# One group of resident blocks instead of two, and an earlier, smaller first table of units

## The chip, the cores and the metric

The kernel runs on one core of a Trainium2 chip. Its time is the device time of one execution in microseconds (us); of several runs the median is given. Engines are named as in the profile: PE is the tensor engine's matmul (PEld its weight load), ACT the scalar engine, DVE the vector engine, POOL the GpSimd engine, and SP the engine that issues most of the transfers.

## The reference

A gated linear recurrence over four sequences of 3648 tokens with 256 channels, and a two-level mixture of experts on its output (4 groups of 4 experts, one expert for each token):

```python
# B, S, D = 4, 3648, 256
a_base = 1.0 / (1.0 + np.exp(-a_param))
log_a = 8.0 * sigmoid(r_gate) * np.log(np.clip(a_base, 1e-06, 1.0 - 1e-06))
a_t = np.exp(log_a)
x_gated = np.sqrt(np.maximum(1.0 - a_t * a_t, 1e-06)) * sigmoid(i_gate) * x
for t in range(S):
    h = a_t[:, t] * h + x_gated[:, t]
    y[:, t] = h
# x = y.reshape(14592, 256)
g_idx = argmax(x @ w_group);  g_w = softmax weight of g_idx
for each group g, for its tokens xg:
    e_idx = argmax(xg @ w_expert[g]);  e_w = softmax weight of e_idx
    for each expert e of the group, for its tokens:      # w1: 256x1024, w2: 1024x256
        out[tokens] = (g_w * e_w) * (relu(x @ w1[g, e]) @ w2[g, e])
```

## The kernel before

The tokens come in 16 chunks of up to 1024 (`SIZES`: 4, then 13 times 8, then 4 and 2 tiles of 128 tokens); chunks are counted from 0 in the code and by words (first, second) in the text. A chunk is loaded with channels on the partitions in two halves. ACT computes tanh (`tanh_r`), exp (`decay`), square, square root (`norm`) and the input gate (`gate_i`) for each half; DVE multiplies (`gated`, `scale_s`) and runs the recurrence (`scan`). Square root and exp need different tables on ACT, so each change of function costs a table load.

*Rows.* PE turns the scanned chunk to rows of tokens and computes the routing logits in the same products (`rows1`, two tiles of 128 tokens to a call: eight products on PE's timeline, 128x148 each). They land in PSUM, and ACT copies them to SBUF (`rows2`). The PSUM has eight banks: `q_r` has two buffers of one bank, `q_h` two of one bank, `q_y` and `q_o` one buffer of two banks each; the rows take `q_y` and `q_o` in turn.

*Routing.* DVE finds each token's expert and its place in the expert's list (`route1`, `route3`, `weigh`, `route4`; ACT's `route2` is an exponential over d_; PE's `rank` counts over tiles with tri and ones; pi holds the places). POOL then writes the rows to the lists in DRAM (`scatter`, tensor y_s), one indirect transfer for each tile.

*Blocks and units.* Work on experts starts before all tokens are routed. (1) Four experts (0, 4, 8, 12, `RES`) have their weights resident. After the chunks in `RSTAGES` a block of up to 128 tokens of each is computed in plain fp32 (`add_blocks`: `rows_block` is the gather that SP issues, `turn_block`, `copy_block`, `mm1_block`, `relu_block`, `mm2_block`, `finish_block`, `give_block`). (2) After the chunks in `STAGES` a table is made on DVE of so many units, a unit being 256 tokens of one expert (`early`, `table`, then three small products on PE, `in_row1`, and `in_row2` on DVE). Its entries are registers for SP: which weights to load, which rows to gather. The first 12 units (`add_native`) split w1 into two parts in fp32r (`split_halves`: ACT makes w1h, DVE w1l) and take w2 in plain fp32; later ones (`add_unit`) split both. A unit's rows are gathered by SP (`gather`, g<-y_s), turned by PE (`turn_native`), copied by ACT (xh) and DVE (xl, `rest_halves`). (3) After the last chunk a table of pairs follows (`tP`, the number of its units is fixed at `NPS`), and (4) a tail for each of the 16 experts, of two blocks of 128 tokens or three, by the count that is left. The buffers of the resident weights become those of the units' weights.

*Order.* Each engine's order is fixed when the program is built: `Plan.run` places every operation by a model with a cost for each operation, a hop between engines (`HOP`, `hop`), a rate and delays for transfers, buffers that come free (`Ring`), and a due time (SOON is at once). Operations of one engine, and the transfers issued by SP and POOL, run in the order in which the plan placed them. `order=` adds an order without data.

In the profile all matmuls but the transposes have the line of the helper `matmul`: L249.

Of the kernel before, what the change touches and what calls it, by code (L numbers as in the profile page):

```python
# [45 lines left out]
class Plan:  # L46


    HOP = 0.14
    RATE, LAG, FAR = 400e3, 2.0, 4.0  # L50
    COOL, WARM = 2.7, 3.4
    TABLE, TURN = 1.28, 2.0
    SLACK, RUSH = 0.02, 0.3
# [24 lines left out]
        return o  # L78

    def hop(self, a, b):  # L80
        return self.HOP if a.dma or a.engine != b.engine else 0.0 if a.engine == "PE" else 0.1

    def ready(self, ring):
        if len(ring.given) < ring.n:
# [19 lines left out]
    def place(self, o, t):  # L104
        e, us = o.engine, o.cost
        if e == "ACT" and o.table and o.table != self.table:
            us, self.table = us + self.TABLE, o.table
        if e == "PE":
            if t - self.clock[e] > self.COOL:
                self.cold = self.WARM  # L110
            us += min(us, self.cold / 2)
            self.cold = max(0.0, self.cold - us)
        end = self.clock[e] = t + us
        if o.dma:
            self.wire = max(self.wire, end) + o.dma / self.RATE
            end = self.wire + self.LAG if e == "SP" else end + self.FAR
        for b in o.new:
            b.ring.given.append(b)
        for b in o.new + o.use:
            b.left -= 1  # L120
            b.free = max(b.free, end + self.HOP)
        for n in o.next:
            n.wait -= 1
        for n in o.then:
            n.wait -= 1
            n.at = max(n.at, end + self.hop(o, n))
# [31 lines left out]
def rglru_moe_kernel(ctx: ExitStack, tc: tile.TileContext, x, r_gate, i_gate, a_param,  # L158
# [20 lines left out]
    SIZES = [4] + [8] * 13 + [4, 2]   # L179
    CH = 8  # L180

    RES, RSTAGES = (0, 4, 8, 12), (1, 2)
    STAGES = [(4, 8), (7, 9), (10, 9)]
    NATIVE = 12
    HALVES = range(0, NATIVE)

# [17 lines left out]
    STEP2, STEPB, STEPN = 10.5, 7.2, 13.4  # L204
    FIRST = range(1, 5)
    URGENT = (0, 1, 2, 3, 4, 7)
    ORES = 60
    HASTE, SPLIT, PREP, WAHEAD = 8, 8, 12, 25
    IF = 0.3

# [17 lines left out]
    def buf(n):  # L228
        return Buf(rings[n])
# [18 lines left out]
    def matmul(*a, **k):  # L248
        last[0] = T.matmul(*a, **k).ins.name  # L249
# [139 lines left out]


    def rows1(ck, i):
        q = ck.t["qy", i] = pools[ck.qy(i)].tile([P, 2, 512], F32, name=ck.qy(i))
        for k in range(2):
            for h in range(2):
                matmul(q[:, k, h * P:h * P + YW], lhsT=ck.t["a", h][:, (2 * i + k) * P:(2 * i + k + 1) * P],
                         rhs=yw[:, h, :], start=h == 0, stop=h == 1, skip_group_check=True)

    def rows2(ck, i):
        if i % 2 == 0:
            ck.t["yo", i // 2] = pools["wf"].tile([P, 4 * DW], F32, name="wf").rearrange("p (k c) -> p k c", c=DW)  # L400
        S.copy(ck.t["yo", i // 2][:, i % 2 * 2:i % 2 * 2 + 2, :], ck.t["qy", i][:, :, 0:DW])  # L401
# [143 lines left out]
    def act(n):  # L545
        return 0.16 + n / 1180
# [4 lines left out]
    def add_chunk(ck, before):  # L551
        K, W, due, b = ck.K, ck.W, ck.due, ck.b
        ld = {}
        for what in "asx":
            for h in range(2):
                if ck.c:
                    at = due + LOADS[what] + 3 * h
                    ld[what, h] = op("SP", 0.06, lambda what=what, h=h: load(ck, what, h), at,
                                     new=[b[what, h]], dma=W * P * 4, soon=at - AHEAD)
                else:  # L560
                    ld[what, h] = None
                    b[what, h].ring.given.append(b[what, h])
        sq = {}
        for h in range(2):
            th = op("ACT", act(W), lambda h=h: tanh_r(ck, h), due + h * OTURN, [ld["a", h]], use=[b["a", h]], table="exp")
            de = op("ACT", act(W) + 0.18, lambda h=h: decay(ck, h), due + h * OTURN, [th], use=[b["a", h]], table="exp")
            sq[h] = op("ACT", act(W), lambda h=h: square(ck, h), due + h * OTURN, [de], [b["v", h]], [b["a", h]])
            if ck.c < 2:
                plan.either(sq[h], "DVE", dve(W), lambda h=h: square(ck, h, True))
        n2 = op("ACT", 2 * act(W), lambda: norm(ck), due + ONORM, [sq[0], sq[1]], use=[b["v", 0], b["v", 1]], table="sqrt")  # L570
        ga = []
        for h in range(2):
            gi = op("ACT", act(W), lambda h=h: gate_i(ck, h), due + OGATE, [ld["s", h]], use=[b["s", h]], table="exp")
            ga.append(op("DVE", dve(W), lambda h=h: gated(ck, h), due + OGATED, [gi, ld["x", h]], use=[b["s", h], b["x", h]]))
        ck.sc = []
        for h in range(2):
            ms = op("DVE", dve(W), lambda h=h: scale_s(ck, h), due + OSCAN + OH * h, [ga[h], n2], use=[b["s", h], b["v", h]])
            sc = op("DVE", 0.1 + W / 455, lambda h=h: scan(ck, h, before), due + OSCAN + 1 + OH * h,
                    [ms] + ([before.sc[h]] if before else []), use=[b["a", h], b["v", h]] + ([before.b["a", h]] if before else []))
            ck.sc.append(sc)  # L580

        urgent = SOON if ck.c in URGENT else 0.0
        rdue = due + OROWS + (SOON if ck.c in FIRST else 0.0) + (ck.c == 0) * STEP1
        ck.qy = lambda i: "q_o" if ck.c < 6 and i % 2 else "q_y"
        ck.y, yos, r1s = [], [], []
        r0 = []
        u = K / CH
        early = ck.c <= STAGES[-1][0]

        def at(o):  # L590
            return due + (ROUTE if early else o) + urgent
        for i in range(K // 2):
            q = buf(ck.qy(i))
            r1 = op("PE", 1.1, lambda i=i: rows1(ck, i), rdue + 2 * i, ck.sc, [q], [b["a", 0], b["a", 1]])
            if i % 2 == 0:
                yos.append(buf("wf"))
            yo = yos[-1]
            r2 = op("ACT", 0.62, lambda i=i: rows2(ck, i), rdue + 2 * i, [r1], [yo] if i % 2 == 0 else [], [q] + ([yo] if i % 2 else []),
                    order=ACTWF[-1:])
            ACTWF.append(r2)  # L600
            ck.y.append(r2)
            if i % 2 == 1 or i == K // 2 - 1:
                r1s.append(chain(route1(ck, i // 2), [0.23, 0.23], at(OROUTE[0]), ck.y[i // 2 * 2:] + r1s[:1],
                                 [b["d"]] if i < 2 else [], [yo] + ([b["d"]] if i >= 2 else []))[1])
                ck.routed = plan.ops[-2]
                r0.append(op("POOL", 0.25, lambda i=i // 2: rows3(ck, i), at(OROUTE[0]), r1s[-1:], use=[yo]))
        r3a, r3 = chain(route3(ck), [0.32, 0.31, 0.32, 0.38, 0.42, 0.17], at(OROUTE[2]), r1s, [b["oe"]], [b["d"]])
        r2 = op("ACT", 0.34, lambda: route2(ck), at(OROUTE[1]), [r3a], (), [b["d"]], table="exp")
        _, rw = chain(weigh(ck), [0.31, 0.18, 0.18, 0.17, 0.15, 0.3], at(OROUTE[2]) + OW, [r2, r3], use=[b["d"]] + yos)
        q = buf("q_y")  # L610
        rk = op("PE", 0.15, lambda: rank(ck), at(ORANK), [r3, before and before.acc], [q], [b["oe"]], order=[before and before.hold])
# [85 lines left out]
    def in_row2(tb, n):  # L697
        q = tb.q
        er = small([1, n])
        tb.act = small([1, n], I32)  # L700
        V.tensor_scalar(er, q[0:1, :n], float(NE - 1), None, op0=ALU.min)
        yield
        V.tensor_scalar(tb.act, q[0:1, :n], float(NE) - 0.5, None, op0=ALU.is_lt)
        yield
        tb.ei = small([1, n], I32)
        V.tensor_copy(tb.ei, er)
        yield
        tb.chg = small([1, n], I32)
        V.tensor_tensor(tb.chg[:, 2:], er[:, 2:], er[:, :n - 2], op=ALU.not_equal)
# [758 lines left out]
```

## Time and profile before

| | us |
|---|---|
| median of 3 runs | 899.62 (898.64 to 902.72) |
| profiled execution, its own time | 901.76 |
| its span, first to last instruction | 900.0 |
| busy: PE, DVE, ACT, POOL | 833.2, 656.4, 606.8, 307.0 |
| first product of unit 0 on PE | 149.13 |
| first results of units 0, 11, 36 on ACT | 168.63, 348.72, 648.18 |
| first result of the last tail | 888.36 |

Busy PE time is modelled, since products are pipelined: the step from the start of one row to the start of the next says what a product costs. A row of the timeline gives start, duration, engine, line, operation, out<-in, shape, the count that was merged, and in brackets the idle time of the engine ahead of it with what ended it. Positions in time are microseconds from the first instruction.

### The profile page before, as it was taken

The page shows a single profiled execution, that of the slowest core. Times are in us where ns is not written, and L with a number is a line of the kernel's source. Part 1 is how long each engine was busy: PE and PEld are TensorE (multiplying, and loading weights), DVE is VectorE, ACT ScalarE, POOL GpSimd, SP SyncE. Part 2 cuts the span into 40 slices and gives each one's busy share as a digit, 9 for nine tenths or more (in the row PEclk, how much of TensorE's full clock was granted, in tenths as well). Part 3 has the DMA queues.
Part 4 walks back from the last instruction along what each step waited for, and adds up shares of the span by engine and source line. Part 5 has one row for each costly group of instructions (what it writes and reads, how often), then busy time and mean ns, then how long its engine had stood idle before and what let it go on. Part 6 is the DMA issues. An engine that isn't in the chain of part 4 may idle for free.

```text
span 900.0 us, 18908 instructions
## 1 busy us (share of the span) xinstructions
PE 833.2 (93%) x6274; PEld 809.9 (90%) x6274; DVE 656.4 (73%) x1345; ACT 606.8 (67%) x901; POOL 307.0 (34%) x290
## 2 busy tenths in 40 slices
PE   2348999999999999999999999999999999999994
PEld 1238998999999899999999999999999999999994
DVE  5796888888889766887777777767766667666681
ACT  8996999999999736556565555556554555555561
POOL 2255753672863467321111111111211213122132
PEclk9968999999999999999999999999999999999997
DMA  9979968988977468857677677688665556555420
GB/s 301 419 286 395 343 224 304 414 302 325 401 264 275 159 240 275 261 180 251 218 232 228 221 232 230 221 273 268 196 190 173 178 183 209 153 178 180 136 72 23
DMA packets 74462, 216.28 MB, mean 240 GB/s; under 512 B 10709, under 2 KB 28895, under 8 KB 71776
## 3 DMA queue, kind: packets, MB, share of 16 engines
q1 hardware_dynamic: 62464, 183.61, 61.4%
q0 software_dynamic: 11872, 31.10, 9.0%
q8 instruction: 66, 1.08, 0.5%
q14 instruction: 60, 0.49, 0.2%
HBM read 182.76 MB, written 34.00 MB: 241 GB/s over the span
## 4 chain that ended last, share of the span: by engine, by line
PE 79%; DMA 6%; ACT 6%; issue 6%; DVE 2%; POOL 1%; SPq 0%; POOLq 0%; DVEq 0%; ACTq 0%
PE q_o L249 37%; PE q_h L249 29%; PE q_y L249 9%; PE q_r L889 2%; DMA a<-in_r_gate_dram 1%; POOL out_dram L1011 1%; DMA i<-in_i_gate_dram 1%; DMA x<-in_moe_w_dram 1%; ACT v L367 1%; ACT wf L401 1%; DMA x<-in_x_dram 1%; DMA y_s<-wf,pi 1%; DMA out_dram<-o,cl 1%; ACT L367 1%; ACT a L348 1%
## 5 line engine op out<-in xcount | busy, mean ns | idle before, releaser
L1011 POOL DMA_INDIRECT out_dram<-o,cl x122 | 138.1, 1132 | 439.0 <-ACT o L1003 240.7
L249 PE MATMUL q_h<-xh,w1h 128*128 128x256 f32 (+1 forms) x720 | 191.2, 294 | 1.5 <-ACT xh L1131 1.5
L502 POOL DMA_INDIRECT y_s<-wf,pi x114 | 145.8, 1279 | 84.0 <-issue 37.9
L249 PE MATMUL q_h<-xl,w1h 128*128 128x256 f32 x592 | 166.8, 282 | 0.0
L249 PE MATMUL q_h<-xh,w1l 128*128 128x256 f32 x592 | 166.8, 282 | 0.0
L249 PE MATMUL q_o<-w2h,hh 128*128 128x256 f32 x784 | 158.2, 334 | 1.2 <-DVE o L1005 0.8
L249 PEld LDWEIGHTS q_o<-w2h,hh 128*128 128x128 f32 x784 | 124.7, 190 | 9.3 <-DVE o L1005 1.0
L249 PEld LDWEIGHTS q_h<-xh,w1h 128*128 128x128 f32 x720 | 128.6, 193 | 2.5 <-ACT xh L1131 1.7
L917 ACT ACTIVATE hh<-q_h 128x512 fp32r<-128x512 f32 x100 | 60.1, 602 | 92.7 <-PE q_h L249 82.7
L249 PEld LDWEIGHTS q_h<-xl,w1h 128*128 128x128 f32 x592 | 111.7, 189 | 0.6
L249 PEld LDWEIGHTS q_h<-xh,w1l 128*128 128x128 f32 x592 | 111.7, 189 | 0.0
L920 DVE SCALAR_TENSOR_TENSOR hl<-q_h,hh 128x512 fp32r<-128x512 f32 x100 | 68.8, 688 | 48.3 <-ACT hh L917 48.1
L249 PE MATMUL q_y<-yw,a 128*128 128x148 f32 x368 | 59.3, 305 | 33.4 <-DVE a L388 25.4
L249 PEld LDWEIGHTS q_y<-yw,a 128*128 128x128 f32 x368 | 53.7, 201 | 36.9 <-issue 19.8
L249 PE MATMUL q_o<-w2l,hh 128*128 128x256 f32 x464 | 78.7, 295 | 0.0
L249 PEld LDWEIGHTS q_o<-w2l,hh 128*128 128x128 f32 x464 | 66.4, 188 | 1.4
L388 DVE TENSOR_TENSOR_SCAN a<-a,v 128x1024 f32<-128x1024 f32 (+8 forms) x38 | 67.4, 1791 | 0.0
L868 DVE TENSOR_TENSOR w1l<-x,w1h 128x1024 fp32r<-128x1024 f32 x50 | 61.0, 1220 | 6.7 <-ACT w1h L866 4.8
L249 PE MATMUL q_o<-w2h,hl 128*128 128x256 f32 x400 | 64.4, 283 | 0.0
L917 ACT ACTIVATE a<-q_y 128x384 fp32r<-128x384 f32 (+1 forms) x64 | 24.9, 442 | 57.3 <-issue 29.5
L1005 DVE TENSOR_SCALAR o<-q_o,cl 128x256 f32<-128x256 f32 x53 | 25.6, 483 | 51.6 <-ACT o L1003 33.4
L868 DVE TENSOR_TENSOR w2l<-x,w2h 128x1024 fp32r<-128x1024 f32 x50 | 60.5, 1216 | 2.8 <-ACT w2h L866 2.8
(336 smaller groups left out, 1861.7 us busy)
## 6 DMA issues: line engine op xcount, KB each, us to landing
x<-in_moe_w_dram SPq DMA_DIRECT2D x100, 512.0 KB, 4.6
wf<-in_moe_w_dram SPq DMA_DIRECT2D x64, 512.0 KB, 4.0
w2h<-in_moe_w_dram SPq DMA_DIRECT2D x14, 1024.0 KB, 8.0
a<-in_r_gate_dram SPq DMA_DIRECT2D x26, 512.0 KB, 9.6
i<-in_i_gate_dram SPq DMA_DIRECT2D x26, 512.0 KB, 9.1
x<-in_x_dram SPq DMA_DIRECT2D x26, 512.0 KB, 8.9
w2l<-in_moe_w_dram SPq DMA_DIRECT2D x24, 512.0 KB, 7.9
g<-y_s SPq DMA_DIRECT2D x37, 276.0 KB, 4.5
```

Of the source, the lines that this page charges most:

```text
L249: last[0] = T.matmul(*a, **k).ins.name
L348: S.activation(a, a, AF.Tanh, scale=0.5)
L367: S.activation(v, v, AF.Sqrt, scale=-0.25, bias=quarter)
L388: V.tensor_tensor_scan(a[:, sl], a[:, sl], v[:, sl], init, ALU.mult, ALU.add)
L401: S.copy(ck.t["yo", i // 2][:, i % 2 * 2:i % 2 * 2 + 2, :], ck.t["qy", i][:, :, 0:DW])
L502: ins = G.indirect_dma_start(out=y_s, out_offset=bass.IndirectOffsetOnAxis(ap=ck.pi[:, k:k + 1], axis=0), in_=ck.t["yo", k // 4][:, k % 4, ...
L868: V.tensor_tensor(lo[m.b][:, sl], src, hi[m.b][:, sl].bitcast(F32), op=ALU.subtract)
L889: T.transpose(m.qx[:, h * P:(h + 1) * P], m.g[:, h, c * X1:c * X1 + P], ident)
L917: S.activation(hh, q, AF.Relu)
L920: V.scalar_tensor_tensor(hl, q, 0.0, hh.bitcast(F32), op0=ALU.max, op1=ALU.subtract)
L1005: V.tensor_scalar(o, m.qo[h], m.col("cw", h), None, op0=ALU.mult)
L1011: ins = G.indirect_dma_start(out=out, out_offset=bass.IndirectOffsetOnAxis(ap=m.col("idx", h), axis=0), in_=m.o[h], in_offset=None, bounds ...
```

## The change

`RSTAGES` loses the second group of four blocks (after the third chunk). `STAGES` puts a table of two units after the fourth chunk and one of six after the fifth, in place of eight after the fifth; the later tables of nine stay. `NPS` grows by two, which keeps the number of token places: four blocks fewer, two units more. The second chunk's rows (`SPREAD`) use `q_y` and `q_o` for the first four tiles and two single banks each of `q_h` and `q_r` for the last four, so ACT copies those in four pieces. Ahead of them PE gets four products of 296 columns whose result is not used (`warm`), due once the scale of the second half is done. The third chunk's square root on ACT is ordered behind the second chunk's routing exponential. A few figures of the planner's model differ: the hop on one engine, when a POOL transfer has landed, the cost of a scatter of the first four chunks, the due time of the blocks.

```diff
-    RATE, LAG, FAR = 400e3, 2.0, 4.0
+    RATE, LAG, NEAR, FAR = 400e3, 2.0, 2.4, 4.0
...
-        return self.HOP if a.dma or a.engine != b.engine else 0.0 if a.engine == "PE" else 0.1
+        return self.HOP if a.dma or a.engine != b.engine else 0.0 if a.engine == "PE" else 0.04
...
         if o.dma:
+            far = end + self.NEAR + min(self.FAR, max(0.0, self.wire - end))
             self.wire = max(self.wire, end) + o.dma / self.RATE
-            end = self.wire + self.LAG if e == "SP" else end + self.FAR
+            end = self.wire + self.LAG if e == "SP" else far
...
-    RES, RSTAGES = (0, 4, 8, 12), (1, 2)
-    STAGES = [(4, 8), (7, 9), (10, 9)]
+    RES, RSTAGES = (0, 4, 8, 12), (1,)
+    STAGES = [(3, 2), (4, 6), (7, 9), (10, 9)]
...
-    NPS = 37 - NA
+    NPS = 39 - NA
...
-    ORES = 60
+    ORES = 55
+    HEAT = 4
+    SPREAD = (1,)
...
     def rows1(ck, i):
-        q = ck.t["qy", i] = pools[ck.qy(i)].tile([P, 2, 512], F32, name=ck.qy(i))
+        n = ck.qy(i)
+        q = ck.t["qy", i] = ([pools[n].tile([P, 512], F32, name=n) for _ in range(2)] if n in ("q_h", "q_r") else
+                             pools[n].tile([P, 2, 512], F32, name=n))
...
+    def warm(n):
+        q = pools["q_r"].tile([P, 512], F32, name="q_r")
+        for _ in range(n):
+            matmul(q[:, 0:2 * YW], lhsT=ident, rhs=yw.rearrange("p h w -> p (h w)"), start=True, stop=True)
...
-        S.copy(ck.t["yo", i // 2][:, i % 2 * 2:i % 2 * 2 + 2, :], ck.t["qy", i][:, :, 0:DW])
+        q, k = ck.t["qy", i], i % 2 * 2
+        if type(q) is list:
+            for n in range(2):
+                S.copy(ck.t["yo", i // 2][:, k + n, :], q[n][:, 0:DW])
+        else:
+            S.copy(ck.t["yo", i // 2][:, k:k + 2, :], q[:, :, 0:DW])
...
-        n2 = op("ACT", 2 * act(W), lambda: norm(ck), due + ONORM, [sq[0], sq[1]], use=[b["v", 0], b["v", 1]], table="sqrt")
+        n2 = op("ACT", 2 * act(W), lambda: norm(ck), due + ONORM, [sq[0], sq[1]], use=[b["v", 0], b["v", 1]], table="sqrt",
+                order=[before.exps] if ck.c == 2 else ())
...
+        if ck.c == 1:
+            plan.op("PE", 0.5 * HEAT, lambda: warm(HEAT), due + OSCAN + SOON, [ms], [buf("q_r")])
...
-        ck.qy = lambda i: "q_o" if ck.c < 6 and i % 2 else "q_y"
+        ck.qy = lambda i: ("q_h", "q_r")[i % 2] if ck.c in SPREAD and i > 1 else "q_o" if ck.c < 6 and i % 2 else "q_y"
...
-            ck.sca.append(op("POOL", 1.3 * n, ...
+            ck.sca.append(op("POOL", (1.65 if ck.c < 4 else 1.3) * n, ...
```

What this does to the order shows in three places. In each name the last number tells buffers apart; w1h_175 to w2l_182 are the resident weights of the four experts, w1 and w2 of each.

First, PE from the third chunk's rows to the first product of block 0 (rows are products of yw and a; tri and ones are the rank; hl is a block's gathered rows). Before:

```order
L249 MATMUL q_y<-yw,a 128x148 x4
L249 MATMUL q_o<-yw,a 128x148 x4
L249 MATMUL q_y<-yw,a 128x148 x4
L249 MATMUL q_o<-yw,a 128x148 x4
L249 LDWEIGHTS tri
L249 MATMUL q_y<-cn,tri 128x16
L249 LDWEIGHTS ones
L249 MATMUL q_y<-cacc,ones 128x16
L1127 MATMUL q_r<-yw,hl 128x128 x4
L249 LDWEIGHTS ones
L249 MATMUL q_y<-cacc,ones 128x16
L249 MATMUL q_h<-xh,w1h_175 128x128 x8
```

After:

```order
L252 MATMUL q_o<-yw,a 128x148 x4
L252 MATMUL q_y<-yw,a 128x148 x4
L252 MATMUL q_o<-yw,a 128x148 x4
L252 MATMUL q_y<-yw,a 128x148 x4
L252 MATMUL q_o<-yw,a 128x148 x4
L252 LDWEIGHTS tri
L252 MATMUL q_y<-cn,tri 128x16
L252 LDWEIGHTS ones
L252 MATMUL q_y<-cacc,ones 128x16
L1146 MATMUL q_r<-yw,hl 128x128 x4
L252 MATMUL q_h<-xh,w1h_175 128x128 x16
```

The third chunk's rank and block 0 now stand behind the fourth chunk's four groups of rows as well, which came within block 0 before.

Second, PE ahead of unit 0 (its first product is the one with w1h_1408, now w1h_974; g is a unit's gathered rows, t are the table's columns). Before:

```order
L249 MATMUL q_h<-xh,w2h_181 128x128 x16
L249 MATMUL q_y<-yw,a 128x148 x4
L249 MATMUL q_o<-w2l_182,hh 128x256 x4
L249 LDWEIGHTS tri
L249 MATMUL q_y<-cn,tri 128x16
L249 LDWEIGHTS ones
L249 MATMUL q_y<-cacc,ones 128x16
L249 MATMUL q_o<-w2l_182,hh 128x256 x4
L249 MATMUL q_h<-xh,w1h_1408 128x256
```

After:

```order
L252 MATMUL q_o<-w2l_182,hh 128x256 x8
L252 LDWEIGHTS tri
L252 MATMUL q_y<-cn,tri 128x16
L252 LDWEIGHTS ones
L252 MATMUL q_y<-cacc,ones 128x16
L1102 MATMUL q_r<-yw,g 128x128 x8
L252 LDWEIGHTS ones
L252 MATMUL q_y<-cacc,ones 128x16
L252 MATMUL q_y<-yw,t_1192 1x128
L252 MATMUL q_y<-yw,t_1193 1x128
L252 MATMUL q_y<-yw,t_1213 128x128
L252 MATMUL q_h<-xh,w1h_974 128x256
```

Between block 3 and unit 0 there stand now the fifth chunk's rank, the turns of units 0 and 1, and the count and the row products of the fifth chunk's table.

Third, DVE ahead of unit 0's xl, the last operand of its first products. Before:

```order
L388 SCALAR_TENSOR_TENSOR a<-a,v 128x640
L388 SCALAR_TENSOR_TENSOR a<-a,v 128x384
L1057 TENSOR_TENSOR w1l_1436<-w2l_1379,w1h_1408 128x1024
L526 TENSOR_TENSOR cl<-g,mA_1249 128x4
L527 TENSOR_SCALAR cl<-cl 128x2
L1065 TENSOR_TENSOR xl<-q_r,xh 128x512
```

After:

```order
L702 SCALAR_TENSOR_TENSOR t_1193<-t_1192,t_1193 128x1
L703 TENSOR_SCALAR t_1193<-t_1193 128x1
L784 TENSOR_TENSOR t_1221<-t_1186,t_1190 128x16
L786 TENSOR_SCALAR t_1221<-t_1221 128x16
L788 TENSOR_TENSOR t_1221<-t_1221,t_1186 128x16
L790 SCALAR_TENSOR_TENSOR done<-t_1221,done 128x16
L1084 TENSOR_TENSOR xl<-q_r,xh 128x512
```

The table of the fifth chunk, 24 steps of which the last six are shown, now stands directly ahead of xl.

More of the change, by code (lines that the diff above doesn't have):

```diff
@@ L391, in rows1 @@
     def rows1(ck, i):
-        q = ck.t["qy", i] = pools[ck.qy(i)].tile([P, 2, 512], F32, name=ck.qy(i))
+        n = ck.qy(i)
+        q = ck.t["qy", i] = ([pools[n].tile([P, 512], F32, name=n) for _ in range(2)] if n in ("q_h", "q_r") else
+                             pools[n].tile([P, 2, 512], F32, name=n))
         for k in range(2):
             for h in range(2):
-                matmul(q[:, k, h * P:h * P + YW], lhsT=ck.t["a", h][:, (2 * i + k) * P:(2 * i + k + 1) * P],
+                matmul((q[k] if type(q) is list else q[:, k])[:, h * P:h * P + YW], lhsT=ck.t["a", h][:, (2 * i + k) * P:(2 * i + k + 1) * P],
                          rhs=yw[:, h, :], start=h == 0, stop=h == 1, skip_group_check=True)
+    def warm(n):
+        q = pools["q_r"].tile([P, 512], F32, name="q_r")
+        for _ in range(n):
+            matmul(q[:, 0:2 * YW], lhsT=ident, rhs=yw.rearrange("p h w -> p (h w)"), start=True, stop=True)
     def rows2(ck, i):
@@ L592, in add_chunk @@
         for i in range(K // 2):
-            q = buf(ck.qy(i))
-            r1 = op("PE", 1.1, lambda i=i: rows1(ck, i), rdue + 2 * i, ck.sc, [q], [b["a", 0], b["a", 1]])
+            q = [buf(ck.qy(i)) for _ in range(1 + (ck.qy(i) in ("q_h", "q_r")))]
+            r1 = op("PE", 1.1, lambda i=i: rows1(ck, i), rdue + 2 * i, ck.sc, q, [b["a", 0], b["a", 1]])
             if i % 2 == 0:
@@ L597, in add_chunk @@
             yo = yos[-1]
-            r2 = op("ACT", 0.62, lambda i=i: rows2(ck, i), rdue + 2 * i, [r1], [yo] if i % 2 == 0 else [], [q] + ([yo] if i % 2 else []),
+            r2 = op("ACT", 0.62 + 0.1 * (len(q) - 1), lambda i=i: rows2(ck, i), rdue + 2 * i, [r1], [yo] if i % 2 == 0 else [], q + ([yo] if i % 2 else []),
                     order=ACTWF[-1:])
@@ L607, in add_chunk @@
         r3a, r3 = chain(route3(ck), [0.32, 0.31, 0.32, 0.38, 0.42, 0.17], at(OROUTE[2]), r1s, [b["oe"]], [b["d"]])
-        r2 = op("ACT", 0.34, lambda: route2(ck), at(OROUTE[1]), [r3a], (), [b["d"]], table="exp")
+        ck.exps = r2 = op("ACT", 0.34, lambda: route2(ck), at(OROUTE[1]), [r3a], (), [b["d"]], table="exp")
         _, rw = chain(weigh(ck), [0.31, 0.18, 0.18, 0.17, 0.15, 0.3], at(OROUTE[2]) + OW, [r2, r3], use=[b["d"]] + yos)
@@ L617, in add_chunk @@
             step = [] if n == 1 else None
-            ck.sca.append(op("POOL", 1.3 * n, lambda k=k, step=step: scatter(ck, range(k, k + n), step), at(OSCAT), [r4, rw] + r0,
+            ck.sca.append(op("POOL", (1.65 if ck.c < 4 else 1.3) * n, lambda k=k, step=step: scatter(ck, range(k, k + n), step), at(OSCAT), [r4, rw] + r0,
                              use=[b["pi"], yos[k // 4]], dma=n * P * DW * 4, order=ck.sca[-1:]))
@@ L707, in in_row2 @@
         yield
-        tb.chg = small([1, n], I32)
-        V.tensor_tensor(tb.chg[:, 2:], er[:, 2:], er[:, :n - 2], op=ALU.not_equal)
+        if n > 2:
+            tb.chg = small([1, n], I32)
+            V.tensor_tensor(tb.chg[:, 2:], er[:, 2:], er[:, :n - 2], op=ALU.not_equal)
         yield
```

## The prediction

> **What bounds the kernel now.** I read the page first: busy times and slices.
>
> ```profile
> PE 833.2 (93%) x6274; PEld 809.9 (90%) x6274; DVE 656.4 (73%) x1345; ACT 606.8 (67%) x901; POOL 307.0 (34%) x290
> ...
> PE   2348999999999999999999999999999999999994
> ```
>
> TensorE (PE) is full from the fourth slice on. The table by stretches gives the change-over (columns: stretch, its length, then busy us and count of PE, PEld, DVE, ACT, POOL; granted clock, DMA share, GB/s):
>
> ```profile
> 33.00:103.00 70.00, 45.81 (x280) 41.47 (x280) 56.73 (x140) 61.96 (x77) 41.70 (x34) 0.80 0.93 362
> 149.00:200.00 51.00, 51.00 (x355) 47.97 (x354) 41.44 (x107) 47.87 (x62) 36.14 (x32) 1.00 0.92 349
> 149.00:888.00 739.00, 734.68 (x5660) 720.13 (x5658) 538.81 (x1061) 470.45 (x738) 234.40 (x215) 1.00 0.69 226
> ```
>
> From 33 to 103 us ACT is busy for 62.0 of 70 us and PE for 45.8; from 149 us, where unit 0 begins, PE idles for 4.3 us in 739. So the end is the start of unit 0 plus the PE work that lies behind it, and that is my sum. The sum is made against the profiled execution (901.76 us, span 900.0); the median of the runs shown is 899.62, and the difference that I find is applied to that median.
>
> **PE work taken away and added.** The timeline of PE, within the two groups of blocks and up to unit 0:
>
> ```profile
> 77.12 1.89 PE L249 MATMUL q_o<-w1l,hh 128*128 128x256 f32 x8
> ...
> 81.68 3.58 PE L249 MATMUL q_o<-w1l,hh 128*128 128x256 f32 x8 [2.45 <-ACT hh L1143]
> ...
> 118.91 3.62 PE L249 MATMUL q_o<-w1l,hh 128*128 128x256 f32 x16
> 122.36 3.73 PE L249 MATMUL q_h<-xh,w2h 128*128 128x128 f32 x32
> 125.93 1.17 PE L249 MATMUL q_y<-yw,a 128*128 128x148 f32 x8
> 126.94 3.62 PE L249 MATMUL q_o<-w2l,hh 128*128 128x256 f32 x16
> ...
> 134.97 0.60 PE L1083 MATMUL q_r<-yw,g 128*128 128x128 f32 x4
> 135.41 1.17 PE L249 MATMUL q_y<-yw,a 128*128 128x148 f32 x8
> ...
> 149.13 0.47 PE L249 MATMUL q_h<-xh,w1h 128*128 128x256 f32 x1
> ```
>
> A resident block costs 3.45 (118.91 to 122.36) + 3.57 (to 125.93), and its turn half of a unit's 0.44 (134.97 to 135.41): 7.25 us. Four fewer take 29.0 us off PE. A group of rows is 1.0 us (125.93 to 126.94).
>
> ```profile
> L1003 ACT ACTIVATE o<-q_o,cl x19: 473/474/475, 434.5 to 648.2; 128x256 f32<-128x256 f32 x19
> ...
> 664.07 0.87 PE L249 MATMUL q_o<-w2h,i 128*128 128x256 f32 x6
> 664.77 0.52 PE L249 MATMUL q_h<-x,w1h 128*128 128x384 f32 x2
> 665.13 0.34 PE L249 MATMUL q_h<-x,w1l 128*128 128x384 f32 x1
> 665.31 0.51 PE L249 MATMUL q_h<-x,w1h 128*128 128x384 f32 x2
> ...
> L249 PE MATMUL q_h<-x,w1h 128*128 128x384 f32 x144 | 37.9, 344 | 0.0
> ```
>
> The first row is each unit's first result: 18 steps in 213.7 us, 11.87 us a unit. The static count of pair units rises by two (39 less 26, not 37 less 26): 23.7 us on PE. Their four output scatters replace those of the four blocks; their weights, splits and gathers lie beside a PE that is full while DVE and ACT are not (last row above), so I cost them at nothing. That cover would be gone only if ACT rose from 470 to 739 us there.
>
> The tails change too, by data. An expert's last rows go to a tail of two or three blocks of 128, three if the blocks left are odd in number. The row x144 counts 16 products for each three-block tail, so there are nine. From the reference's inputs I count the rows that the blocks take off experts 0, 4, 8 and 12: 200, 173, 193, 208 with two groups, 128, 105, 75, 97 with one; of 619, 887, 1054 and 1305 tokens, that makes expert 4's tail longer and shortens those of experts 8 and 12: eight. A third block is 24 products more of 256 columns at 0.118 (six in 0.70 from 664.07) and 48 that are 384 wide at 0.18 (three in 0.54 from 664.77): 2.8 + 2.8 = 5.6 us less.
>
> Behind unit 0 also come the six groups of rows that stood ahead of it (four of the sixth chunk, two of the seventh): +5.9; unit 1's turn moves ahead: -0.4. PE work behind unit 0: 23.7 - 5.6 + 5.9 - 0.4 = **+23.6 us**.
>
> **When unit 0 can begin.** Taken away are 29.0 + 5.9 - 0.4 = 34.5 us ahead of it; were all else equal it would begin at 149.13 - 34.5 = 114.6. Whether it can, the lists of the other engines say. ACT, waits and means in the stretch 33 to 103:
>
> ```profile
> ACT a L348 <- DMA a<-in_r_gate_dram: 3.9, 1, 3.9
> ACT hh L1143 <- PE q_h L249: 1.7, 3, 1.2
> ACT wf L401 <- PE q_y L249: 1.4, 3, 0.6
> ACT wf L401 <- PE q_o L249: 0.7, 2, 0.4
> ...
> L353 ACT ACTIVATE a<-a,la 128x1024 f32<-128x1024 f32 x7 | 8.7, 1237 | 0.0
> L348 ACT ACTIVATE a<-a 128x1024 f32<-128x1024 f32 x7 | 7.4, 1052 | 3.9 <-DMA a<-in_r_gate_dram 3.9
> L1143 ACT ACTIVATE hh<-q_h 128x512 f32<-128x512 f32 x6 | 3.6, 597 | 1.7 <-PE q_h L249 1.7
> ...
> 36.01 1.28 ACT L367 ACT_TABLE_LOAD   x1
> 37.31 2.19 ACT L367 ACTIVATE v<-v,la 128x1024 f32<-128x1024 f32 x2
> ...
> 102.60 0.34 ACT L423 ACTIVATE d__963<-d__963 128x160 f32<-128x160 f32 x1
> ```
>
> The last row is the fifth chunk's routing exponential. ACT idles 7.7 us on the way to it (the four waits). The new list has ahead of the same instruction one tanh, exp and square more (3.3 us), two relus (1.2), two weight splits (2.1; a split is a pass over 128x1024 like tanh, 1.05), and the second chunk's copies in four pieces for two, with one block copy less, which I let cancel: 6.6, and 6.1 with the overlap of neighbours (the groups of this view sum to 67.4 where ACT is busy for 62.0). With no wait left the exponential comes at 102.6 - 7.7 + 6.1 = 101.0, with all of them at 108.7. I take 3.2 of wait, so 104.2: the 3.9 on the load goes, since the SP queue stands behind the blocks' gathers, which wait for the second chunk's scatters, and these start 2.9 us sooner: ACT's last copies of its rows stood behind the table load and the roots of 36.01 to 39.4, 3.4 us, and now stand ahead of them (the smaller pieces give back some 0.5); the waits for rows stay.
>
> Are the warm-up products worth anything? Four products of 296 columns are 2 us at full rate, 4 us cold, in time in which PE idles for the scans, so they cost nothing. With or without them ACT takes the first copy of that chunk only after the first chunk's exponential, so I give them 0 to 0.7 us, inside the 2.9. The Trainium skill (TensorE: Matmul & The Clock Gate, Part 1) says that full rate comes only after some 3.4 us of sustained work in a free-running window, so by it the rows may still start cold; my sum would lose 0.7 us at most.
>
> Now DVE, POOL and SP around the routing (the last column of the gather's row is the median from issue to landing):
>
> ```profile
> 65.58 0.14 DVE L494 CAST pi<-pos 128x8 int32<-128x8 f32 x1
> 103.39 0.21 DVE L451 CAST cn<-inc 128x16 bf16<-128x16 f32 x1
> 109.65 0.15 DVE L733 COPY sm<-q_y 128x16 f32<-128x16 f32 x1
> 113.98 0.17 DVE L771 SCALAR_TENSOR_TENSOR done<-t,done 128x16 f32<-128x16 f32 x1
> 138.06 0.69 DVE L1065 TENSOR_TENSOR xl<-q_r,xh 128x512 fp32r<-128x512 f32 x1
> ...
> 66.50 2.28 POOL L502 DMA_INDIRECT y_s<-wf,pi  x1 [4.54 <-DVE pi L494]
> 79.16 0.98 POOL L502 DMA_INDIRECT y_s<-wf,pi  x1 [0.30 <-issue]
> 87.64 1.87 POOL L502 DMA_INDIRECT y_s<-wf,pi  x1 [7.25 <-issue]
> 102.11 0.98 POOL L502 DMA_INDIRECT y_s<-wf,pi  x1 [0.30 <-DVE m__962 L441]
> ...
> g<-y_s SPq DMA_DIRECT2D x37, 276.0 KB, 4.5
> ```
>
> The new order puts the fifth chunk's table (L733 to L771, 24 steps, 4.5 us) ahead of unit 0's rest xl on DVE, and its three row products ahead of unit 0's first product on PE. So: exponential 104.2; counts cast about 1 later; PE ends block 3 (blocks from about 70, since the fourth chunk's copies now stand before the first block's on ACT; four blocks 29.0, the fifth chunk's rows 4, other 3.5) at 106.6; rank, both units' turns and counts to 107.9; DVE is through the positions at 109.0, the table at 113.5, xl at 114.2; PE adds its three products, about 0.5 of it behind xl: 114.7. The other route: the third chunk's positions come 5.3 us later than 65.58, since its rank now stands behind the fourth chunk's rows; eight scatters are 13.6 us (66.50 to 80.14), the fourth chunk's follow at once: 71.8 + 13.6 + 0.3 + 13.6 = 99.3; SP's gather about 2 later, the second 1.2 behind it, 4.5 to land: 107.0. It is hidden by block 3 with 0.9 us to spare. For some ten hand-overs from engine to engine, which this walk takes at no cost, I allow 1.5 (no row gives it: 0 to 3): **116.2**. Ends: 111.5 (exponential at 101.0) and 121 (108.7 and the hand-overs).
>
> PE idles 6 us ahead of unit 0 then. The rows 77.12 and 81.68 are the same eight products, 1.89 us, and 3.58 after 2.45 us of idling: **+1.7** for unit 0's start. In units 0 to 2 ACT's list (65 instructions by such means) is 55 us of durations, 51 with overlap, against 51 of PE's (three units of 13 and twelve groups of rows); in the row 149 to 200 it is 47.9 against 51.0 and PE loses nothing. So 0 to 4 us of new waits; I take **+1.5**.
>
> Sum: (116.2 - 149.13) + 23.6 + 1.7 + 1.5 = **-6.1 us**: 899.62 - 6.1 = **893.5 us**. The rest (costs of hops, of scatters and of landing in the planner) issues nothing and only moves order; where PE is full it is covered by PE.
>
> **Rivals.**
> *Slower: the scatter queue.* The 16 scatters before unit 0's gather have 0.9 us of room; beyond it each us moves turns, counts, table and unit 0 alike. At 1.71 us each (13.64 over eight) they hide. At the rate of the slowest eight shown (87.64 to 103.09, 15.45) unit 0 is 2.8 later. They decide from 2.15 us each on, where the 6.1 are gone; at 2.5 they take 12.7 more, less 0.9, and the kernel ends near 905. Only single ones are that slow here. Chance 0.09. The Trainium skill (SBUF — State Buffer, Who interferes with whom) has DVE operations with two SBUF inputs and GpSimd's SBUF reads exclude each other, which speaks for it: DVE runs scans and the table meanwhile. The uneven scatters of one size, 0.98 to 2.28 us, agree; that they are of one cause no row shows.
> *No change that can be measured: ACT keeps its waits.* If ACT idles all 7.7 us again, unit 0 is 4.5 later: 898.0. The waits for rows speak for it, the earlier SP queue against. Chance 0.28, with any mix that stays within 0.5% (4.5 us, about what a measurement of this kernel tells from no change).
> *More gain: no wait on ACT, none after unit 0.* Unit 0 at 112.5, no new waits: 888.3. The scatters' 107.0 speaks against much more. Chance 0.20.
>
> **How the numbers follow.** My forecast, 890 to 895, has 0.43. Faster by over 0.5%: 0.43 + 0.20 = 0.63; within: 0.28; slower: 0.09. The range leaves one tenth on each side: from 885 (unit 0 at its early end, no waits, some cold start gone) to 902 (its late end and 4 us of waits). The likeliest case alone spans 890 to 895.
>
> **What would show it.** PE's first product of unit 0 near 116, with an idle of about 6 us ahead of it put down to DVE; 11.9 us a unit and 27 such units before the tails; 128 and not 144 products of q_h with 384 columns; the fifth chunk's exponential on ACT near 104; no wait of 3.9 us for a load. I am wrong if the wait ahead of unit 0 is for its gather, if PE idles by more than 4 us between units 0 and 8 (the eighth chunk's table or ACT late), or if unit 0 begins after 121.

## The result: slower, 1.0075 of the time before

The kernel before took 899.64 us in this comparison (median of six runs, 898.64 to 902.72), the changed kernel 906.60 us (904.93 to 909.23): a ratio of 1.0075, 95% interval 1.0057 to 1.0093. The forecast was 893.5 with a range of 885 to 902. The profiled execution of the changed kernel took 905.02 us, 3.3 more than that of the kernel before, while the medians lie 7.0 apart; the traces can account for the 3.3 only. A ratio is estimated from the undisturbed executions of both kernels, so it need not be the exact quotient of the medians beside it.

The page of the changed kernel, busy times and PE's slices:

```profile
PE 829.1 (92%) x6264; PEld 804.8 (89%) x6264; DVE 665.6 (74%) x1375; ACT 608.5 (67%) x905; POOL 306.7 (34%) x290
...
PE   2359799798999999999999999999999999999994
```

PE has less to do than before (829.1 us for 833.2) and is full later: three slices behind the first 9 are at 7, 7 and 8, where before all were at 9 from the fifth to the last but one. The timeline of PE around the start of unit 0:

```profile
105.83 0.17 PE L252 MATMUL q_y<-cn,tri 128*128 128x16 bf16 x1
...
109.63 0.38 PE L252 MATMUL q_y<-yw,t 128*1 128x128 f32 x2 [2.39 <-DVE t L678]
111.59 1.31 PE L252 MATMUL q_y<-yw,t 128*1 128x128 f32 x4 [1.58 <-DVE t L703]
112.56 0.56 PE L252 MATMUL q_h<-xh,w1h 128*128 128x256 f32 x1
...
119.60 0.70 PE L252 MATMUL q_o<-w2h,hh 128*128 128x256 f32 x2 [1.84 <-ACT hh L1118]
```

Unit 0 starts at 112.56, not 149.13: 36.6 us earlier, and still the kernel ends later. The table by stretches (columns as in the prediction) says where the time went; the first two rows are of the kernel before (unit 0 to unit 11's result, and from there to the last tail), the others of the changed kernel, for the same stages and for the worst 30 us:

```profile
149.00:349.00 200.00, 197.83 (x1328) 185.25 (x1327) 159.00 (x413) 165.94 (x233) 120.12 (x112) 0.99 0.82 295
349.00:889.00 540.00, 537.12 (x4335) 534.95 (x4333) 379.94 (x649) 304.98 (x507) 114.27 (x104) 1.00 0.64 200
```

```profile
112.00:334.00 222.00, 209.88 (x1361) 194.65 (x1361) 182.76 (x441) 189.93 (x257) 125.78 (x111) 0.96 0.83 295
180.00:210.00 30.00, 25.01 (x138) 21.94 (x139) 21.19 (x51) 19.57 (x24) 18.95 (x18) 0.86 0.75 263
334.00:892.00 558.00, 556.33 (x4524) 554.37 (x4522) 390.66 (x689) 312.60 (x523) 126.97 (x116) 1.00 0.63 197
```

The same twelve units with what lies between them take 222 us for 200, and PE idles 12.1 us in them for 2.2. Around 180 to 210 even ACT is busy for only 19.6 of 30 us, and the granted clock is 0.86. From unit 11's result on, the 18 us more are the work that was added (540 to 558).

The lists of POOL, DVE, ACT and PE in that place, put together by time from the timelines (y_s is a scatter of routed rows, out_dram the scatter of a unit's results, which are in a tile o):

```profile
158.23 0.99 POOL L517 DMA_INDIRECT y_s<-wf,pi  x1 [5.25 <-DVE w1l L1076]
158.46 0.45 ACT L1022 ACTIVATE o<-q_o,cl 128x256 f32<-128x256 f32 x1
...
173.69 0.98 POOL L1030 DMA_INDIRECT out_dram<-o,cl  x1 [0.30 <-issue]
174.98 0.98 POOL L517 DMA_INDIRECT y_s<-wf,pi  x1 [0.30 <-issue]
176.27 0.98 POOL L1030 DMA_INDIRECT out_dram<-o,cl  x1 [0.30 <-issue]
...
180.44 0.48 DVE L1024 TENSOR_SCALAR o<-q_o,cl 128x256 f32<-128x256 f32 x1 [3.11 <-DMA out_dram<-o,cl]
180.98 3.78 PE L252 MATMUL q_o<-w2h,hh 128*128 128x256 f32 x8 [4.96 <-DVE o L1024]
...
197.57 0.98 POOL L517 DMA_INDIRECT y_s<-wf,pi  x1 [0.30 <-issue]
198.86 1.11 POOL L1030 DMA_INDIRECT out_dram<-o,cl  x1 [0.30 <-issue]
200.27 2.03 POOL L1030 DMA_INDIRECT out_dram<-o,cl  x1 [0.30 <-issue]
205.09 0.47 ACT L1022 ACTIVATE o<-q_o,cl 128x256 f32<-128x256 f32 x1 [4.50 <-DMA out_dram<-o,cl]
205.61 3.68 PE L252 MATMUL q_o<-w2h,hh 128*128 128x256 f32 x8 [3.70 <-ACT o L1022]
```

Read it from the top. Unit 1's result is out of PSUM at 158.9 (ACT, second row). Its scatters stand on POOL behind nine scatters of routed rows, and one more stands between them: they go out at 173.69 and 176.27. There are three tiles o (`BUFS`), so unit 2's second result needs the tile of one of these two. It waits on DVE until 180.44, by the times for the scatter of 173.69: from issue to landing these take 6.2 to 7.2 us in this stretch. PE needs q_o, a single PSUM buffer, for the next unit: it idles 4.96 us, and the eight products that follow take 3.78 us for 1.89. The same happens again with unit 2's scatters (198.86, behind 14 scatters of routed rows), unit 3's result on ACT (205.09) and PE (205.61). These two stalls are 8.7 of the 12.1 us in which PE idles. Another 1.8 are the wait at 119.60, for a relu that stands on ACT behind two weight splits whose loads came late (ACT idles 1.28 and 0.83 us for them).

### The profile page after: what moved, and what is told of

The parts are those of the page before. It is cut to its first block, busy times and chain, and to the rows that moved or that the text cites. A ratio compares the mean times of both kernels' runs of the same rounds, so it can differ in the third digit from the quotient of the medians.

```text
span 903.0 us, 18968 instructions
## 1 busy us (share of the span) xinstructions
PE 829.1 (92%) x6264; PEld 804.8 (89%) x6264; DVE 665.6 (74%) x1375; ACT 608.5 (67%) x905; POOL 306.7 (34%) x290
## 4 chain that ended last, share of the span: by engine, by line
PE 63%; issue 16%; DMA 7%; ACT 6%; POOL 4%; DVE 3%; SPq 0%; POOLq 0%; ACTq 0%; DVEq 0%
PE q_o L252 30%; PE q_h L252 25%; PE q_y L252 6%; POOL out_dram L1030 4%; DMA w2l<-in_moe_w_dram 3%; PE q_r L908 2%; DMA out_dram<-o,cl 1%; DMA a<-in_r_gate_dram 1%; DMA i<-in_i_gate_dram 1%; ACT v L370 1%; DVE a L391 1%; ACT i L374 1%; ACT a L356 1%; ACT L370 1%; DMA x<-in_x_dram 1%
## 5 line engine op out<-in xcount | busy, mean ns | idle before, releaser
L1030 POOL DMA_INDIRECT out_dram<-o,cl x126 | 144.1, 1143 | 453.5 <-ACT o L1022 221.3
L252 PE MATMUL q_o<-w2h,hh 128*128 128x256 f32 x816 | 167.1, 337 | 10.9 <-DVE o L1024 5.0
L252 PE MATMUL q_h<-xl,w1h 128*128 128x256 f32 x624 | 176.9, 283 | 0.0
L252 PE MATMUL q_h<-xh,w1l 128*128 128x256 f32 x624 | 176.5, 283 | 0.0
L252 PEld LDWEIGHTS q_o<-w2h,hh 128*128 128x128 f32 x816 | 131.1, 192 | 20.4 <-DVE o L1024 5.1
L252 PEld LDWEIGHTS q_h<-xl,w1h 128*128 128x128 f32 x624 | 118.6, 190 | 0.9 <-DVE xl L1084 0.2
L939 DVE SCALAR_TENSOR_TENSOR hl<-q_h,hh 128x512 fp32r<-128x512 f32 x108 | 74.4, 689 | 60.0 <-ACT hh L936 58.3
L252 PEld LDWEIGHTS q_h<-xh,w1l 128*128 128x128 f32 x624 | 118.5, 190 | 0.0
L252 PE MATMUL q_o<-w2h,hl 128*128 128x256 f32 x432 | 69.6, 283 | 0.0
L936 ACT ACTIVATE a<-q_y 128x256 fp32r<-128x256 f32 (+1 forms) x64 | 24.6, 435 | 55.4 <-issue 31.0
```

What stands on the lines that cost most here:

```text
L936: S.activation(hh, q, AF.Relu)
L939: V.scalar_tensor_tensor(hl, q, 0.0, hh.bitcast(F32), op0=ALU.max, op1=ALU.subtract)
L1030: ins = G.indirect_dma_start(out=out, out_offset=bass.IndirectOffsetOnAxis(ap=m.col("idx", h), axis=0), in_=m.o[h], in_offset=None, bounds ...
```

## The experiments

Each run is given as a ratio to the kernel before on the same chip. That kernel took 899.6, 900.4 and 900.1 us in three of the comparisons and 913.4, 910.6 and 913.3 in the other three; what these chips do is told in the last section. A run is compared with the changed kernel beside it where there is one.

Three theories. Theory 1: the results of early units run into POOL's queue of scatters, and three tiles o are too few. Theory 2: ScalarE (ACT) sets the pace there, and the tile is where it shows. Theory 3: the planner's new figures make a bad order.

**Five tiles.** A native unit's second result goes to another pool of two (the tiles hl, which these units don't use):

```diff
-        o = m.o[h] = pools["o"].tile([P, D], F32, name="o")
+        o = m.o[h] = (pools["hs"].tile([P, 512], F32, name="hl")[:, 0:D] if m.native and h else pools["o"].tile([P, D], F32, name="o"))
```

> The changed kernel, but the second result tile of each native unit comes from a pool of two that is idle there, so that five result tiles stand where three did; the planned order stays. Theory 1 (result tiles: a unit's results wait for an earlier unit's output scatter, which stands behind routing scatters on POOL): the waits of 3.11 us on DVE at 180.44 and 4.50 us on ACT at 205.09 go, with them PE's gaps of 4.96 and 3.70 us and the slow first products behind each (1.9 and 1.8 us): 906.6 - 12.4 = 894, between 892 and 897. Theory 2 (ScalarE and VectorE have too much to do beside units 0 to 3, and the result tile is only where it shows): the gaps move to another tile, 904 to 907.

The same edit in the kernel before:

> The kernel before with the same five result tiles. Its units 0 to 3 show no wait of a result for a scatter, so theory 1 expects no change: 899.6, within 1.5 us. If five tiles gain 3 us or more here too, the tiles are worth something for another reason, and the first run says less about the change.

Measured: 1.0073 (1.0048 to 1.0097) and 1.0056 (1.0033 to 1.0078), on a chip of the slower kind. The control failed: the edit by itself costs, so the first run settles nothing. In the kernel before PE now idled 2.59 and 2.96 us at 358 and 370 us, where the first pair units use hl themselves; that they wait for the borrowed tiles is likely, not shown (the profile names no releaser for the first wait, and a tile hl for the second). So the edit was kept to units 0 to 8 (`and m.u < 9`), with the changed kernel beside it:

> The changed kernel once more, as the anchor for the runs beside it on the same chip: 0.4 to 1.1% slower than the kernel before (1.0075 in the first comparison). Every theory expects this; a ratio outside it would say that the chip matters more than the change.

> Five result tiles again, but the two borrowed ones only for units 0 to 8, so that the pair units that own that pool later do not wait for it. Theory 1 (result tiles behind the scatter queue cost about 12 us): 10 to 13 us below the changed kernel beside it. Theory 2 (up to the last chunks ScalarE and the chunks' other work set how far the units get, and the result tile is only where the lack shows): within 3 us of the changed kernel, with the result of unit 11 at the same time as there.

Measured: 1.0174 (1.0144 to 1.0204) for the changed kernel and 1.0090 (1.0064 to 1.0117) with five tiles, 926.72 and 918.42 us: 8.3 us less, short of the 10 to 13 that theory 1 had and clear of the 3 of theory 2. The changed kernel was far outside of what was expected of it on this chip, so the pair was repeated:

> The changed kernel beside the next three, on their chip: 1.0075 of the kernel before where PE does not crawl in the blocks at 80 to 95 us, 1.017 where it does.

> Five result tiles for units 0 to 8, order kept. Theory 1: the waits of DVE and ACT for a result tile at 180 and 205 us are gone and the run is 8 to 12 us faster than the changed kernel beside it (8.3 in the first pair, on a chip that was slower throughout). If that first difference came from the crawl and not from the tiles: within 3 us.

> Five result tiles for units 0 to 8 in the changed kernel once more. On a chip where the kernel before takes 900 us the changed kernel is at 1.0075; the two pairs gave 0.991 and 0.990 of it, so 0.997 to 1.000 of the kernel before is expected if the tiles explain the loss there too, 1.005 or more if the loss there has another cause.

Measured: 1.0173 (1.0139 to 1.0208) and 1.0087 (1.0063 to 1.0110), 9.1 us less; and with five tiles on a chip where the kernel before takes 900.11 us 0.9969 (0.9955 to 0.9983). The changed kernel did not run beside that one; against its 1.0075 in the first comparison it is 0.0106 of 900 us, 9.5 us. With two tiles more the change is a small gain. The chain of waits of that last run, 150 to 215 us, has no wait of DVE or ACT for out_dram any more; what PE waits for now is:

```profile
PE q_r L1102 <- DMA g<-y_s: 3.1, 1, 3.1
...
PE q_o L252 <- DVE hl L1024: 1.8, 1, 1.8
```

A unit's gather has taken the place of the second stall, so a part of the loss is handed on.

The traces place the gain. The first results of units 0 and 11, in the first profile of the changed kernel and then with five tiles on that last chip:

```profile
134.79 0.47 ACT L1022 ACTIVATE o<-q_o,cl 128x256 f32<-128x256 f32 x1
...
334.08 0.47 ACT L1022 ACTIVATE o<-q_o,cl 128x256 f32<-128x256 f32 x1 [1.07 <-PE q_o L252]
```

```profile
132.93 0.47 ACT L1022 ACTIVATE o<-q_o,cl 128x256 f32<-128x256 f32 x1
...
327.00 0.47 ACT L1022 ACTIVATE o<-q_o,cl 128x256 f32<-128x256 f32 x1 [1.07 <-PE q_o L252]
```

From the one result to the other it takes 199.3 us and 194.1, so 5.2 less; in the two pairs on the slower chips it is 5.3 less (205.7 and 200.4) and 9.4 less (209.8 and 200.4). Another 1.9 us of the last run lie ahead of unit 0's result, where no result waits for a tile: its PE does not have the wait for late weights there. So the tiles themselves are worth some 5 to 9 us. The forecast was 0.993 of the kernel before; what makes up the 3 us that five tiles still lack no run shows by itself.

**ACT's load.** The first half of each native unit's split is made twice:

```diff
-            S.copy(m.w["h"][:, sl], m.w[0][:, sl])
+            for _ in range(2 - k):
+                S.copy(m.w["h"][:, sl], m.w[0][:, sl])
```

> The changed kernel with the first half of each native unit's weight split done twice on ScalarE, 1.05 us more in each of 12 units, nothing else. Theory 2 (ScalarE sets the pace there): 8 to 12 us slower than the changed kernel. Theory 1 (ScalarE has slack and waits for result tiles): at most 3 us slower.

Measured: 925.11 us, 1.0159 (1.0127 to 1.0191), beside 926.72 for the changed kernel. ACT is busy 11.3 us longer (619.0 for 607.7) and the kernel is not slower. Nor is a cost hidden by PE's other waits on these chips (last section): unit 0's first result comes at 147.4 (145.7 beside it), and from there to unit 11's it takes 205.1 us for 205.7. Theory 2 falls: ACT has that much slack there, as long as it waits for result tiles.

**The figures.** The changed kernel with the old figures, and the kernel before with the new ones:

> The changed kernel with the planner's old figures (a fixed 4.0 us until a scatter has landed, 0.1 us between instructions of one engine, 1.3 us for every routing scatter); stages, blocks and the spread rows stay. Theory 3 (the new figures give the order in which results and routing scatters stand badly): 892 to 897. Theories 1 and 2: the early start of unit 0 among the routing scatters is the cause whatever the figures are: 902 to 909.

> The kernel before with only the planner's new figures. Theory 3: slower than before, 903 to 908. Theories 1 and 2: the units come 36 us later than in the changed kernel whatever the figures are, so no stall of results: 897 to 902.

Measured: 1.0114 (1.0083 to 1.0145) and 1.0010 (0.9991 to 1.0028), on a chip of the slower kind. The new figures alone change nothing that can be told, and with the old ones the new stages are slower than the kernel before all the same: neither of theory 3's forecasts came. Whether the old figures are better or worse in the changed kernel is not settled, since it did not run beside them. Nor does the run with the old figures speak for theory 1: unit 0's first result comes at 155.9 there, 10 us later than in the changed kernel on chips of that kind, and between 100 and 340 us ACT and DVE wait for an output scatter only 2.4 us. It loses its time in another way.

**The parts.** The kernel before with all but the stages (spread rows, warm-up products, figures), and the changed kernel without its warm-up products (`warm(0)`, order kept):

> The kernel before with the spread rows of the second chunk, the warm-up products and the new figures, but with its own stages and two groups of blocks. Theory 1 places the whole loss in the stages: 897 to 903 on a chip where the kernel before takes 899.6, so a ratio of 0.997 to 1.004. If the rows or the figures cost something by themselves: 1.005 or more.

> The changed kernel without its four warm-up products, the order of all else kept. The prediction gave them 0 to 0.7 us, so the time of the changed kernel within 1.5 us. If PE's crawl at 80 to 95 us hangs on where its instructions lie in its list (8 fewer stand ahead), it would move or go: up to 10 us faster than the changed kernel on that chip.

Measured: 0.9980 (0.9966 to 0.9994) and 1.0068 (1.0051 to 1.0086), with 900.44 us before. So the loss is in the stages; the rest is worth 2 us. The warm-up products make no difference that shows; PE did not crawl on this chip, so what they do to that the run can't say.

**The early table.** The two tables of two and six become one of eight behind the fifth chunk; blocks, rows and figures stay:

```diff
-    STAGES = [(3, 2), (4, 6), (7, 9), (10, 9)]
+    STAGES = [(4, 8), (7, 9), (10, 9)]
```

> The changed kernel with one table of eight units behind the fifth chunk in the place of two units behind the fourth and six behind the fifth: unit 0 starts some 9 us later, the amount of work is the same. If the start of unit 0 sets the end (the prediction's sum): 9 us more than the changed kernel. Theory 2: the same time within 3 us, since the units catch up before unit 11. Theory 1: 4 to 9 us less, as the results then come later against the scatters and wait less, or no change where that is lost at the start.

> One table of eight behind the fifth chunk once more, for a profile without disturbance and to see whether its gain repeats. Theory 1 (early results run into the scatter queue): 0.994 to 0.999 of the kernel before again; unit 0 starts 8 to 12 us later than in the changed kernel, and the finishing instructions of units 2 and 3 wait less than 1 us for a result tile. If the gain came from something else (PE crawling in the blocks at 80 to 95 us, as in the other runs of the changed kernel on these chips), the finishing instructions may wait as before, and PE shows no such crawl.

> The same with five result tiles for units 0 to 8. Theory 1: with the later start the scatters are out of the way, so the tiles add nothing: within 2 us of the run beside it. If the later start only made the wait smaller: 3 us or more faster.

Measured: 906.15 us beside 926.72 for the changed kernel, 0.9962 (0.9943 to 0.9981). These 20.6 us are more than any theory had. Again, where the kernel before takes 900.44: 0.9977 (0.9963 to 0.9992), 0.0098 or 8.8 us under the changed kernel's ratio, and 0.9977 (0.9963 to 0.9991) with five tiles. The prediction's own sum, by which a later unit 0 is a later end, had +9 us here. Unit 0's result comes at 146.3, 11.5 us later than in the changed kernel (134.8), and unit 11's at 327.3, 6.8 us earlier (334.1). No result of DVE or ACT waits for an output scatter in that stretch. 158 to 206 us in the changed kernel and in this one, and then unit 1's result and its scatters in this one:

```profile
158.00:206.00 48.00, 38.95 (x248) 35.27 (x247) 34.19 (x95) 36.15 (x47) 35.78 (x32) 0.93 0.79 278
```

```profile
158.00:206.00 48.00, 47.58 (x324) 44.04 (x323) 42.33 (x110) 45.63 (x59) 34.72 (x31) 1.00 0.94 351
...
164.14 0.46 ACT L1022 ACTIVATE o<-q_o,cl 128x256 f32<-128x256 f32 x1
166.92 1.02 POOL L1030 DMA_INDIRECT out_dram<-o,cl  x1 [0.30 <-issue]
168.27 1.89 POOL L1030 DMA_INDIRECT out_dram<-o,cl  x1 [0.16 <-PE q_y L252]
```

POOL is as full in both (35.8 and 34.7 of 48 us, and 0.3 from each transfer to the next on top), yet PE does 47.6 us of work for 39.0. Unit 1's results stand elsewhere in POOL's list: they go out 2.8 us after the result here, 15.2 us after it there. More tiles then add nothing, as theory 1 has it. The planner placed the operations of all engines anew in this run, so it does not show by itself that the place on POOL is what counts.

**The order on POOL.** The changed kernel, an output scatter due 30 us earlier in the planner:

```diff
-            ... lambda h=h, step=step: give(m, h, step), due, [f_], ...
+            ... lambda h=h, step=step: give(m, h, step), due - 30, [f_], ...
```

> The changed kernel with three result tiles, but an output scatter's due time is 30 us earlier in the planner, so that unit 1's and unit 2's output scatters stand among the first routing scatters of their chunk and not behind 12 and 16 of them. Theory 1: the stalls of units 2 and 3 go as with five tiles, 6 to 12 us faster than the changed kernel. If the lack of tiles is only where another lack shows (the routing scatters that now come later): within 3 us.

(In the first profile nine and 14 routing scatters stand ahead, as the rows above show, not 12 and 16.) Measured: 922.73 us, 1.0097 (1.0069 to 1.0126), 7.5 us less than the changed kernel beside it (930.21). But the first stall did not go, it changed its name:

```profile
191.67 0.17 DVE L509 CAST pi<-pos 128x8 int32<-128x8 f32 x1 [4.78 <-DMA y_s<-wf,pi]
191.75 0.48 DVE L1024 TENSOR_SCALAR o<-q_o,cl 128x256 f32<-128x256 f32 x1
192.28 2.08 PE L252 MATMUL q_o<-w2h,hh 128*128 128x256 f32 x4 [5.92 <-issue]
```

Ahead of the result on DVE stands the cast of the next chunk's places, which needs a tile pi that earlier scatters of routed rows still read, and these come later now. The profile names no releaser for PE's 5.92 us; by the times it is the result, which ends at 192.23. So the tile o is one of two things that hang on POOL's list at that place: theory 1 is too narrow with the tile alone. PE's list is that of the changed kernel up to where 200 us stand in its first profile, and planned anew behind that, so the 7.5 us need not be the output scatters' alone.

**A faster version.** The parts that cost nothing with the old stages (a_nostage above), and one figure, an early scatter's cost:

```diff
-            ck.sca.append(op("POOL", (1.65 if ck.c < 4 else 1.3) * n, ...
+            ck.sca.append(op("POOL", (1.5 if ck.c < 4 else 1.3) * n, ...
```

> The kernel before's stages with the spread rows and new figures (0.998 of the kernel before in its run), and the planner's cost of an early routing scatter at 1.5 us in the place of 1.65. Only a try for a faster version: if the planner's order follows its own times as closely as so far, some 4 us faster than that run, 0.993 of the kernel before; if that order depends on more than the figure, 0.997 to 1.002.

> The version that was 0.987 of the kernel before on a chip where that one took 913 us. If that gain is the version's own (its order leaves PE idle less): 0.987 to 0.993 here too. If it came from where the slow chip stalls PE (no crawl in its blocks): 0.995 to 1.000 on a chip where the kernel before takes 900.

Measured: 901.59 us, 0.9867 (0.9848 to 0.9886), where the kernel before takes 913.34, and 895.00 us, 0.9940 (0.9917 to 0.9962), where it takes 900.11. The second lies between its two forecasts. It beats both kernels, though ACT waits 3.4 us for an output scatter in its profile too; why one figure of the planner is worth this was not studied.

## Why the prediction was wrong, by its steps

*The start of unit 0: right, and better than forecast.* 112.56 for 116.2. The fifth chunk's exponential ran at 103.42 (104.2), block 3 ended at 105.83 (106.6). The wait on the table's steps was 2.39 + 1.58 = 4.0 us where 6 stood. ACT's wait for a load fell from 3.9 to 1.3 us:

```profile
ACT a L351 <- DMA a<-in_r_gate_dram: 1.3, 1, 1.3
...
103.42 0.34 ACT L438 ACTIVATE d__1059<-d__1059 128x160 f32<-128x160 f32 x1
```

The rival of the scatter queue ahead of unit 0 did not come about.

*PE's work: right.* The tails fell to eight with three blocks, as this row with 128 products says (x144 before):

```profile
L252 PE MATMUL q_h<-x,w1h 128*128 128x384 f32 x128 | 33.6, 344 | 0.0
```

From unit 11's first result to the last tail's (891.49) it takes 557.4 us for 539.6, 17.8 more where 23.7 - 5.6 = 18.1 was forecast. Unit 0's slow start cost 1.9 us for 1.7: its first nineteen products come 0.21 to 0.22 us apart for the most part, and then 0.12.

*"So 0 to 4 us of new waits; I take +1.5": the step that failed.* From unit 0 to unit 11's result it takes 221.5 us (112.56 to 334.08) for 199.6 (149.13 to 348.72), 21.9 more. The prediction had 5.9 - 0.4 of work, 1.7 and 1.5, so 8.7. By the table of stretches PE idles 12.1 us there for 2.2, 9.9 more, and the two cold restarts are 3.78 - 1.89 and 3.68 - 1.89, 3.7 us: 13.6 us in the place of the 1.5. The step held ACT's list against PE's (51 against 51) and never laid POOL's list beside them; the two long waits were on ACT and DVE, but for what POOL issues, and with their restarts (4.96 + 3.70 + 3.7) they are 12.4 us. The allowance of 4 us was a bound on ACT, not on POOL. The runs with five tiles took 5.2 to 9.4 us out of this stretch; the rest was handed on to other waits, a gather for one, and is not taken apart by a run.

*The sum.* -36.6 for the start, +17.8, +5.5, +1.9 and +13.6 make +2.2 us; the last results lie 3.1 apart (888.36 and 891.49). The prediction's own warning, "if PE idles by more than 4 us between units 0 and 8", is what came.

*The rivals.* The scatter queue was named, but ahead of unit 0, where it had 0.9 us of room. It decided some 60 to 95 us after unit 0's start, through the results' tiles (and, with the output scatters moved, the places), by which the units wait for scatters of chunks that they have nothing to do with.

## What to carry to other kernels

When work is moved earlier, lay out again the list of every engine that it shares with the work it now meets, the transfer queue too, and ask of each small pool (here three result tiles and two tiles of places) when its last reader is issued there, not only how long that takes. A stall that is named after a buffer can hang on the order of a queue: give it another buffer and another order, each by itself, and see whether the wait goes or only changes its name. A longer idle of PE (here 4.96 and 3.70 us) cost twice, the wait and the slow products behind it (1.9 and 1.8 us more).

## What was not expected of the hardware

On the chips where the kernel before takes 910 to 913 us, PE issued the products of the blocks in steps of some 0.7 us or a multiple, with no releaser, in six of seven profiles of the changed kernel and its variants with the same order up to there (five tiles, output scatters earlier); the seventh, with the split made twice, shows two such waits of 3.89 and 2.66 us instead. The four profiles of other orders on such chips have only single ones, the longest of 3.63 us. Here it is in the third run of the changed kernel:

```profile
81.79 0.50 PE L252 MATMUL q_h<-xh,w2h 128*128 128x128 f32 x3 [1.02 <-issue]
83.22 0.60 PE L252 MATMUL q_h<-xh,w2h 128*128 128x128 f32 x2 [0.93 <-issue]
...
91.77 0.37 PE L252 MATMUL q_h<-xh,w2h 128*128 128x128 f32 x1 [1.05 <-issue]
```

In 88 to 95 us PE does seven products there, and 36 in the first profile of the changed kernel (first row); DVE and ACT stand still with it:

```profile
88.00:95.00 7.00, 5.69 (x36) 5.09 (x35) 6.96 (x9) 6.96 (x9) 5.78 (x5) 1.00 1.03 409
```

```profile
88.00:95.00 7.00, 2.08 (x7) 1.23 (x7) 1.62 (x2) 0.26 (x1) 3.94 (x4) 0.50 0.73 246
```

Unit 0's first result comes at 145.2 there, 10 us later than the 134.8 of the first profile. That is about the difference between 1.017 and 1.0075, but it is not shown to be the cause: from unit 0's to unit 11's result it also takes longer there (209.8 us for 199.3), and there is no profile of the kernel before on such a chip. None of the eight profiles from the other chips has a wait of PE without a releaser. What the products wait for is open: no row shows it. It lies outside the first comparison, and both kinds of chip give a like gain of five tiles (medians 8.3 and 9.1 us, and 9.5 across chips).

Eight products were cold after 2.45 us (before), 3.70 and 4.96 us of idling, 3.6 to 3.8 us for 1.89. The Trainium skill (TensorE: Matmul & The Clock Gate, Part 1) has the slow state come after at least one idle window of about 3.4 us. The waits of 3.70 and 4.96 agree with that. The one of 2.45 is shorter and was enough as well, so here the measurement decides.
